# Mirrored row sums, x reversed through DRAM, and a third PSUM bank for the MLP

## The chip, the core and the metric

The kernel runs on one core of one Trainium2 chip. The metric is the device time of one execution in microseconds (us), start to end, as the median of several runs. Profiles are of one execution; their times count from the start of its span. PE is TensorE (matmuls), DVE is VectorE, ACT is ScalarE, POOL is GpSimd, SP is SyncE; the last three also issue DMAs, each from its own queue, in order.

## The reference

A chunked attention is followed by a Fourier mix and an MLP. Batch B = 4, 8 heads, sequence S = 768, head size 64, so 512 columns (DM) per row.

```
for each chunk of 32 rows:                 # keys: 8 memory keys + rows -16..+8 around it
    a = softmax(q_c @ k_full.T / 8);  out[chunk] = a @ v_full
x = out with the heads side by side        # [4, 768, 512]
mixed = real(fft(fft(x, axis=1), axis=2))
u  = x + mixed
un = (u - mean(u)) / sqrt(var(u) + 1e-6)   # over the 512 columns
result = u + relu(un @ w_ch1) @ w_ch2      # w_ch1 [512, 2048], w_ch2 [2048, 512]
```

For a real x, the value of `mixed` at row s and column d equals that at row (768 - s) mod 768 and column (512 - d) mod 512.

## The kernel before

**Tiles.** A batch's x is one SBUF tile `xsb` of 128 partitions x 6 row tiles (st or kt, 0 to 5) x 512 columns, float32. Attention runs in 16 steps, four to a batch, each for two heads: PE turns q and k (`trq`, `trk`, line 313), computes scores in two halves (`sc`, 351), ACT takes the exponential (359), PE the values (`xa`, 372), and DVE divides and writes into `xsb` (`e_norm`, 382 and 383).

**Fourier mix of a batch.** DVE folds x by its symmetries (`e_zy`, `e_pq`, `e_ff`), ACT and DVE split the result into two float16 parts (`e_hi`, `e_lo`), and PE transforms along the sequence into 193 of the frequencies for four parts (`ps`, lines 440 and 534). `e_up` (ACT) and `e_rest` (DVE) copy each part out of PSUM as `up`, in two float16 halves. `e_dn` (DVE, 461) makes a reversed copy `dn` of each part for the row tiles 3 to 5. PE then transforms along the columns, one row tile at a time (`e_columns`, 545): 8 matmuls of 256 columns into one PSUM bank `pm`, from `up` for kt 0 to 2 and from `dn` for kt 3 to 5. `e_sum` (DVE, 551) adds `pm` to x in place, `e_stats` (557, 558) takes mean and variance, `e_un` (ACT, 563) subtracts the mean into a float16 tile, which is transposed into `unT`: by PE in batch 0, by a DMA on SP's queue (`e_flip`, 575) in batches 1 to 3.

**MLP of a batch.** In two halves (sh) of three row tiles: 16 tiles of hidden units `ph` (four matmuls of 384 columns each, 596) go through relu on ACT (`hT`, 603); then for each of the three row tiles 16 matmuls of 512 columns (`pc`, 610, in four parts). `e_osb` (DVE, 616) scales by the row's 1/sigma and adds u, and `e_out` (ACT's queue, 620) stores the 256 KB tile. `e_rstd` (584, 585) computes 1/sigma on POOL.

**PSUM.** Eight banks: one `tr`, two `sc`, one `xa`, two of tag `acc` and two of tag `mlp`. `acc` holds `ps` and `pm`. The MLP's `ph` and `pc` take `mlp` banks in turn; only in the last batch every third of them takes an `acc` bank (`mtag`, 588).

**Order.** All work is handed to a planner (`Plan`, 37) as tasks with an engine, an expected cost, dependences, and the buffers that they take and give back. `order` plays these costs through once, while the program is built, and emits the instructions; on the chip each engine runs its list in that order, with semaphores between engines. MLP matmuls are marked as filler: PE takes them when nothing else is ready. So the Fourier mix and the attention of one batch run between the MLP matmuls of the batch before, and the MLP of batches 2 and 3 is left over at the end. Early on, PE runs `idle` matmuls (654) as a filler.

**Loads.** q and k come on POOL's queue (286) into three buffers each, v on SP's queue (295 to 304) into four, the MLP weights on POOL's queue (786, 790).

Of the kernel before, what the change touches and what calls it, by code (L numbers as in the profile page):

```python
# [10 lines left out]
FP32 = mybir.dt.float32  # L11
# [20 lines left out]
def strided(src, off, dims):  # L32
    return bass.AP(tensor=src.tensor, offset=src.offset + off,
                   ap=[list(src.ap[0])] + [list(d) for d in dims])
# [105 lines left out]
def kernel(  # L140
# [11 lines left out]
    nc = tc.nc  # L152
# [39 lines left out]
    plan = Plan(dict(qs=NS, ks=NS, va=NV, kTb=NKT, qT=2, tr=1, sc=1, xa=1, e1=3,  # L192
                     xsb=3, fold=2, hl=1, up=4, dn=4, acc=2, mlp=2, un=6, unT=2, hT=1, osb=3))
    add = plan.add
# [193 lines left out]

    zy_of, pq_of, ff_of, hl_of, ps_of, up_of, pm_of, un_of, tp_of = ({} for _ in range(9))
    mu_of, unT_of, rstd_of, g_of = {}, {}, {}, {}  # L390
    mid = cpool.tile([P, 2, NST, 1], FP16)
    mid32 = cpool.tile([P, NST, 1], FP32)
    warm = cpool.tile([P, 1], FP32)
    gate = cpool.tile([P, 1], FP32)

# [63 lines left out]
    def e_dn(b, par, ab):  # L459
        dn = fpool.tile([P, 2, HS], FP16, tag="dn", bufs=4, name="dn")  # L460
        nc.vector.tensor_copy(dn, rev_ap(up_of[b, par, ab][2], HS, HS, [[2 * NK, 2]]))
        up_of[b, par, ab][1] = dn

    def g_zy(par, g):
# [84 lines left out]
    def e_sum(b, kt):  # L549
        uv = xs[b][:, kt, :].rearrange("p (j c) -> p c j", c=2)  # L550
        nc.vector.tensor_tensor(uv, pm_of.pop((b, kt)), uv, ALU.add)  # L551

# [19 lines left out]
    def e_flip(b, kt):  # L572
        if kt == 0:
            unT_of[b] = fpool.tile([P, NDT, S], FP16, tag="unT", bufs=2, name="unT")
        nc.sync.dma_start_transpose(unT_of[b][:, :, ts(kt, P)], un_of.pop((b, kt)))

# [9 lines left out]


    def mtag(b, i):
        return "acc" if b == B - 1 and i % 3 == 2 else "mlp"

# [22 lines left out]
    def e_osb(b, sh, stl):  # L613
        st = sh * 3 + stl
        osb_of[b, st] = osb = fpool.tile([P, DM], FP32, tag="osb", bufs=3, name="osb")
        nc.vector.scalar_tensor_tensor(osb, pc_of.pop((b, sh, stl)), rstd_of[b][:, st:st + 1],  # L616
                                       xs[b][:, st, :], ALU.mult, ALU.add)

    def e_out(b, st):
        nc.scalar.dma_start(out[b, ts(st, P), :], osb_of.pop((b, st)))  # L620


    t_zero = add("DVE", 0.2, e_zero, rank=-21)
# [170 lines left out]
    def first_fourier():  # L794
# [38 lines left out]
        return columns_of(0, t_rest)  # L833

    def fourier(b):
        nrm = [[t_norm[b * HP + i, g] for i in ii for g in range(2)] for ii in ((0, 1), (2, 3))]
        t_rest = {}
# [27 lines left out]
    def columns_of(b, t_rest):  # L865
        t_dn = {}
        for par in range(2):
            for ab in range(2):
                t_dn[par, ab] = add("DVE", 0.36, lambda par=par, ab=ab: e_dn(b, par, ab),
                                    [t_rest[par, ab]], take=("dn",))  # L870
        t_un = {}
        allr = list(t_rest.values())
        cols = {}

        def columns(kt):
            cols[kt] = add("PE", 0.9, lambda: e_columns(b, kt),
                           allr + [t_rows] + (list(t_dn.values()) if kt > 2 else []),
                           take=("acc",), rank=len(plan.tasks) + (15 if kt == 3 else 0),
                           give=("up",) * 4 if kt == 2 else ("dn",) * 4 if kt == 5 else ())

        sa = None
        columns(0)
        for kt in range(NST):
            if kt + 1 < NST:
                columns(kt + 1)
            su = add("DVE", 0.7, lambda kt=kt: e_sum(b, kt), [cols[kt]], give=("acc",))
            sa = add("DVE", 0.9, lambda kt=kt: e_stats(b, kt), [su, sa])
            un = add("ACT", 0.72, lambda kt=kt: e_un(b, kt), [sa], take=("un",))
            if b > 0:
                t_un[kt] = add("SP", 0.1, lambda kt=kt: e_flip(b, kt), [un, t_un.get(kt - 1)],  # L890
                               take=("unT",) if kt == 0 else (), give=("un",), moved=0.8,
                               loose=True)
                continue
# [9 lines left out]
    def mlp(b, t_un, rs):  # L903
        for sh in range(2):
            relu = []
            c2 = None
            for ht in range(NHT):
                ph = add("PE", 0.65, lambda sh=sh, ht=ht: e_ch1(b, sh, ht),
                         mlp_prev + [t_un[3 * sh + i] for i in range(3)] + t_w1,
                         take=(mtag(b, ht),), give=("unT",) if sh == 1 and ht == NHT - 1 else (),  # L910
# [5 lines left out]
            for stl in range(3):  # L916
                st = 3 * sh + stl
                for part in range(4):
# [6 lines left out]
                          take=("osb",),   # L925
                          give=(mtag(b, stl), "xsb") if st == NST - 1 else (mtag(b, stl),),
                          rank=RELU(len(plan.tasks)))
                mlp_prev[0] = c2
                add("ACT", 0.1, lambda st=st: e_out(b, st), [os_], give=("osb",), moved=0.9,
                    rank=RELU(len(plan.tasks)))  # L930

    def RELU(i):
        return i - MLPS
# [44 lines left out]
```

## Time and profile before

| | |
|---|---|
| median of 3 runs | 309.21 us (308.92 to 309.44) |
| the profiled execution | 308.85 us, span 307.1 us, granted PE clock 0.999 |
| PE busy | 289.5 us, 3148 matmuls |
| DVE, ACT, POOL busy | 171.2, 161.5, 40.8 us |
| MLP matmuls, ph and pc | 91.6 and 86.9 us of busy PE |
| column matmuls pm | 4 x 9.2 us of busy PE (four groups of 48, 273 ns each) |

The busy time of a matmul runs from its start to its modelled end and overlaps the next one, so the distance from start to start is shorter than the mean duration. A wait is put down to the instruction whose semaphore came last. The time of the profiled execution is its span and what lies around it.

### The profile page before, as it was taken

The page shows a single profiled execution, that of the slowest core. Times are in us where ns is not written, and L with a number is a line of the kernel's source. Part 1 is how long each engine was busy: PE and PEld are TensorE (multiplying, and loading weights), DVE is VectorE, ACT ScalarE, POOL GpSimd, SP SyncE. Part 2 cuts the span into 40 slices and gives each one's busy share as a digit, 9 for nine tenths or more (in the row PEclk, how much of TensorE's full clock was granted, in tenths as well). Part 3 has the DMA queues.
Part 4 walks back from the last instruction along what each step waited for, and adds up shares of the span by engine and source line. Part 5 has one row for each costly group of instructions (what it writes and reads, how often), then busy time and mean ns, then how long its engine had stood idle before and what let it go on. Part 6 is the DMA issues. An engine that isn't in the chain of part 4 may idle for free.

```text
span 307.1 us, 7496 instructions
## 1 busy us (share of the span) xinstructions
PE 289.5 (94%) x3148; PEld 181.5 (59%) x3148; DVE 171.2 (56%) x371; ACT 161.5 (53%) x291; POOL 40.8 (13%) x78
## 2 busy tenths in 40 slices
PE   1399999999999999999989999999999999999994
PEld 1267678866666676666756646675554554554541
DVE  7877895975397887797764399476101001001001
ACT  6656373689884666885257423743360450531710
POOL 8806421132201102000020000000200000000000
PEclk9999999999999999999999999999999999999999
DMA  6989999999944925821361011004201101001011
GB/s 114 197 171 167 204 205 196 198 204 178 193 72 91 203 45 111 136 47 40 89 137 36 2 46 59 0 19 102 86 2 40 64 2 68 34 2 71 31 36 68
DMA packets 60289, 28.93 MB, mean 94 GB/s; under 512 B 48480, under 2 KB 56672, under 8 KB 60256
## 3 DMA queue, kind: packets, MB, share of 16 engines
q1 hardware_dynamic: 47168, 11.61, 21.0%
q0 software_dynamic: 9344, 10.49, 20.8%
q10 hardware_dynamic: 3744, 6.36, 5.7%
q8 instruction: 25, 0.41, 0.5%
q14 instruction: 8, 0.07, 0.1%
HBM read 30.28 MB, written 6.29 MB: 119 GB/s over the span
## 4 chain that ended last, share of the span: by engine, by line
PE 91%; DMA 2%; POOL 2%; DVE 1%; ACT 1%; issue 1%; POOLq 0%; ACTq 0%
PE ph L596 28%; PE pc L610 27%; PE xa L372 9%; PE pm L545 7%; PE ps L440 5%; PE idle L654 5%; PE ps L534 4%; PE sc L351 3%; DMA qs<-in_q_dram 2%; PE trk L313 2%; PE trq L313 2%; DVE osb L616 1%; POOL qs L286 0%; ACT hT L603 0%; PE tp L570 0%
## 5 line engine op out<-in xcount | busy, mean ns | idle before, releaser
L603 ACT ACTIVATE hT<-ph 128x384 f16<-128x384 f32 x128 | 60.9, 492 | 63.0 <-PE ph L596 51.5
L596 PE MATMUL ph<-unT,w_sb 128*128 128x384 f16 x512 | 91.6, 326 | 2.2 <-ACT hT L603 1.1
L610 PE MATMUL pc<-w_sb,hT 128*128 128x512 f16 x384 | 86.9, 379 | 0.0
L596 PEld LDWEIGHTS <-w_sb 128*128 128x128 f16 x512 | 47.8, 97 | 36.8 <-issue 5.7
L616 DVE SCALAR_TENSOR_TENSOR osb<-pc,rstd,xsb 128x512 f32<-128x512 f32 x24 | 18.0, 749 | 82.5 <-PE pc L610 82.4
L610 PEld LDWEIGHTS <-hT 128*128 128x128 f16 x384 | 36.8, 98 | 41.2 <-issue 0.2
L359 ACT ACTIVATE e<-sc,mbias 128x384 f32<-128x384 f32 x64 | 33.8, 583 | 13.8 <-PE sc L351 11.3
L372 PEld LDWEIGHTS xa<-va,e 128*64 128x64 f32 x768 | 25.0, 137 | 7.8 <-issue 7.0
L372 PE MATMUL xa<-va,e 128*64 128x65 f32 x768 | 29.3, 226 | 0.0
L563 ACT ACTIVATE un<-xsb,mu_s 128x512 f16<-128x512 f32 x24 | 17.2, 720 | 14.9 <-DVE mu_s L558 14.8
L382 DVE RECIPROCAL zs<-xa 128x6 f32<-128x6 f32 x32 | 6.1, 191 | 25.6 <-PE xa L372 25.5
L452 ACT CAST up<-ps 128x386 f16<-128x386 f32 x16 | 9.7, 603 | 19.1 <-PE ps L440 13.5
L551 DVE TENSOR_TENSOR xsb<-pm,xsb 128x512 f32<-128x512 f32 x24 | 16.0, 675 | 4.4 <-PE pm L545 4.2
L383 DVE TENSOR_TENSOR xsb<-xa,zs 128x384 f32<-128x384 f32 x32 | 17.8, 557 | 1.1
L557 DVE BATCH_NORM_STATS2 st<-xsb 128x6 f32<-128x512 f32 x24 | 16.4, 684 | 0.5
L654 PE MATMUL idle<-dz 128*128 128x384 bf16 x71 | 15.3, 350 | 1.0 <-DVE zero L230 1.0
L322 ACT COPY qT<-trq 128x768 bf16<-128x768 bf16 x16 | 12.8, 798 | 5.6 <-PE trq L313 5.5
L286 POOL DMA_DIRECT2D ks<-in_k_dram x16 | 10.2, 635 | 35.0 <-PE trk L313 31.4
L584 POOL TENSOR_SCALAR rstd<-mu_s 128x6 f32<-128x6 f32 x4 | 1.0, 245 | 102.0 <-DVE osb L616 57.7
L313 PE MATMUL trq<-ident_b,qs 96*64 96x96 bf16 x256 | 9.4, 221 | 5.1 <-DMA qs<-in_q_dram 5.1
L286 POOL DMA_DIRECT2D qs<-in_q_dram x16 | 10.5, 659 | 25.2 <-PE trq L313 21.5
L456 DVE TENSOR_TENSOR up<-ps,up 128x386 f16<-128x386 f32 x16 | 9.6, 598 | 7.5 <-ACT up L452 7.5
(126 smaller groups left out, 343.5 us busy)
## 6 DMA issues: line engine op xcount, KB each, us to landing
va<-in_v_dram SPq DMA_DIRECT2D x32, 220.0 KB
out_dram<-osb ACTq DMA_DIRECT2D x24, 256.0 KB
w_sb<-in_moe_w_ch_dram POOLq DMA_DIRECT2D x8, 512.0 KB, 16.9
qs<-in_q_dram POOLq DMA_DIRECT2D x16, 192.0 KB, 5.7
ks<-in_k_dram POOLq DMA_DIRECT2D x16, 192.0 KB, 6.1
va<-in_mem_v_dram SPq DMA_DIRECT2D x32, 24.0 KB
va<-in_v_dram SPq DMA_DIRECT2D x32, 22.0 KB
va<-in_v_dram SPq DMA_DIRECT2D x16, 32.0 KB
```

Source lines behind the costliest of these rows:

```text
L286: nc.gpsimd.dma_start(dst[n % NS][0:QP], src[b, 2 * pr:2 * pr + 2].rearrange("h (p j) d -> p h (j d)", j=RB))
L313: nc.tensor.transpose(out_[64 * hh:64 * hh + 64, j * w:(j + 1) * w], src[:, hh, j * D:(j + 1) * D], eye)
L359: nc.scalar.activation(e1[:, :, :, ts(half, 32)], sc[:, :, 0:6, ts(half, 32)], AFT.Exp, bias=mbias[:, half:half + 1], scale=1.0 / math.sqr ...
L372: nc.tensor.matmul(xa[64 * half:64 * half + 64, st, hh, 0:65], e1[:, hh, t6, :], v1[:, hh, 6 * g + t6, 0:65], start=True, stop=True)
L383: nc.vector.tensor_tensor(xs[b][:, 3 * g:3 * g + 3, 2 * pr * D:(2 * pr + 2) * D] .rearrange("p s (h d) -> p s h d", h=2), xa[:, :, :, 0:D] ...
L545: nc.tensor.matmul(pm[:, par, :], lhs, rhs[:, par, :], start=(im == 0), stop=(im == 3))
L563: nc.scalar.activation(un, xs[b][:, kt, :], AFT.Identity, bias=mu_of[b][:, kt, 0:1], scale=-1.0)
L596: nc.tensor.matmul(ph[:, 0:384], w1_sb[:, dt, ts(ht, P)], unT_of[b][:, dt, sh * 384:(sh + 1) * 384], start=(dt == 0), stop=(dt == NDT - 1))
L603: nc.scalar.activation(hT_of[b, sh][:, ht, :], ph_of.pop((b, sh, ht))[:, 0:384], AFT.Relu, bias=0.0, scale=-1.0)
L610: nc.tensor.matmul(pc_of[b, sh, stl], hT_of[b, sh][:, ht, ts(stl, P)], w2_sb[:, ht, :], start=(ht == 0), stop=(ht == NHT - 1))
L616: nc.vector.scalar_tensor_tensor(osb, pc_of.pop((b, sh, stl)), rstd_of[b][:, st:st + 1], xs[b][:, st, :], ALU.mult, ALU.add)
L654: nc.tensor.matmul(fill_of[0][:, 0:384], dz, strided(dz, 0, [[0, 3], [1, P]]), start=True, stop=True)
```

## The change

**Mirrored row sums (batches 1 to 3).** The column transform is done for kt 0 to 2 only, and `e_dn` is gone for these batches. A row tile of the upper half is summed from the `pm` of its mirror, kt - 3, read backwards, and from x, which has been brought into mirrored row order: `e_sum_back` (DVE), a long instruction of 2 x 255 columns and one of two columns. So `xsb` holds the rows 3 to 5 in mirrored order from there on. `e_sum` no longer gives its `acc` bank back; `e_sum_back` of kt + 3 does. The bank's first row is overwritten for row 384, which has no mirror among the first 384, by six matmuls (`e_last_row`) between the sum and the `e_sum_back` of kt 0. The sums run in the order 0, 1, 3, 4, 2, 5.

**x reversed by way of DRAM.** `e_back` writes rows 3 to 5 of `xsb` (786 KB) to a DRAM tensor in reversed partition order, once the batch's last norm is done; `e_mirror` reads it back with four DMAs, shifted by one, into `xr`, which takes the place of `dn`. All five are on POOL's queue.

**Outputs.** The MLP takes the row tiles in the order 0, 3, 4, 5, 1, 2. Tiles 3 to 5 are stored by ACT's queue into a DRAM tensor (`e_out_rows`), and copied from there to their place in mirrored row order by SP's queue (`e_out_back`), with one more DMA for row 384.

**Third bank.** `mtag` gives every third ph or pc tile an `acc` bank in all four batches.

```diff
@@ -190,7 +190,7 @@
     seq = [(b, pr) for b in range(B) for pr in (0, 2, 1, 3)]
 
     plan = Plan(dict(qs=NS, ks=NS, va=NV, kTb=NKT, qT=2, tr=1, sc=1, xa=1, e1=3,
-                     xsb=3, fold=2, hl=1, up=4, dn=4, acc=2, mlp=2, un=6, unT=2, hT=1, osb=3))
+                     xsb=3, fold=2, hl=1, up=4, dn=1, acc=2, mlp=2, un=6, unT=2, hT=1, osb=3))
     add = plan.add
     MLPS = 1000000
 
@@ -386,11 +386,13 @@
             xa[:, :, :, 0:D], zs.unsqueeze(3).to_broadcast([P, 3, 2, D]), ALU.mult)
 
 
-    zy_of, pq_of, ff_of, hl_of, ps_of, up_of, pm_of, un_of, tp_of = ({} for _ in range(9))
+    zy_of, pq_of, ff_of, hl_of, ps_of, up_of, pm_of, un_of, tp_of, dn_of, xr_of = ({} for _ in range(11))
...
+    xd = nc.dram_tensor("x_rows", [2, P, 3, DM], FP32).ap()
+    od = nc.dram_tensor("out_rows", [2, 3, P, DM], FP32).ap()
     gate = cpool.tile([P, 1], FP32)
 
     def e_zy(b, par, c):
@@ -457,9 +459,43 @@
                                 up[:, 0].rearrange("p k s -> p s k"), ALU.subtract)
 
     def e_dn(b, par, ab):
-        dn = fpool.tile([P, 2, HS], FP16, tag="dn", bufs=4, name="dn")
+        if b not in dn_of:
+            dn_of[b] = fpool.tile([P, 4, 2, HS], FP16, tag="dn", bufs=1, name="dn")
+        dn = dn_of[b][:, 2 * par + ab]
         nc.vector.tensor_copy(dn, rev_ap(up_of[b, par, ab][2], HS, HS, [[2 * NK, 2]]))
         up_of[b, par, ab][1] = dn
+
+    def e_back(b):
+        r0 = xd[b % 2, 63:64]
+        nc.gpsimd.dma_start(bass.AP(tensor=r0.tensor, offset=r0.offset,
+                                    ap=[[64 * 3 * DM, 2], [-3 * DM, 64], [1, 3 * DM]]),
+                            xs[b][:, 3:6, :].rearrange("p t d -> p (t d)"))
+
+    def e_mirror(b):
+        xr_of[b] = xr = fpool.tile([P, 3, DM], FP32, tag="dn", bufs=1, name="xr")
+        xb = xd[b % 2]
+        nc.gpsimd.dma_start(xr[1:65], xb[64:128])
+        nc.gpsimd.dma_start(xr[65:128], xb[0:63])
+        nc.gpsimd.dma_start(xr[0:1, 0:2], xb[63:64, 1:3])
+        nc.gpsimd.dma_start(xr[0:1, 2:3], xb[63:64, 0:1])
+
+    def e_last_row(b):
+        pm = pm_of[b, 0]
+        for par in range(2):
+            todo = [(up_of[b, par, ab][0][:, part, HS:HS + 1], (cosD, nsinD)[ab])
+                    for ab in range(2 - par) for part in range(2)]
+            for i, (lhs, rhs) in enumerate(todo):
+                nc.tensor.matmul(pm[0:1, par, :], lhs, rhs[:, par, :], start=(i == 0),
+                                 stop=(i == len(todo) - 1))
+
+    def e_sum_back(b, kt):
+        pm, xr = pm_of.pop((b, kt)), xr_of[b]
+        y = xs[b][:, 3 + kt, :].rearrange("p (j c) -> p c j", c=2)
+        r = xr[:, 2 - kt, :].rearrange("p (j c) -> p c j", c=2)
+        nc.vector.tensor_tensor(y[:, :, 1:HD], strided(pm, HD - 1, [[HD - 1, 2], [-1, HD - 1]]),
+                                r[:, :, 1:HD], ALU.add)
+        nc.vector.tensor_tensor(y[:, :, 0], strided(pm, 0, [[2 * HD - 1, 2]]), r[:, :, 0],
+                                ALU.add)
 
     def g_zy(par, g):
         if g == 0:
@@ -548,7 +584,7 @@
 
     def e_sum(b, kt):
         uv = xs[b][:, kt, :].rearrange("p (j c) -> p c j", c=2)
-        nc.vector.tensor_tensor(uv, pm_of.pop((b, kt)), uv, ALU.add)
+        nc.vector.tensor_tensor(uv, pm_of[b, kt], uv, ALU.add)
 
     def e_stats(b, kt):
         if kt == 0:
@@ -572,7 +608,7 @@
     def e_flip(b, kt):
         if kt == 0:
             unT_of[b] = fpool.tile([P, NDT, S], FP16, tag="unT", bufs=2, name="unT")
-        nc.sync.dma_start_transpose(unT_of[b][:, :, ts(kt, P)], un_of.pop((b, kt)))
+        nc.sync.dma_start_transpose(unT_of[b][:, :, ts(SLOT.index(kt), P)], un_of.pop((b, kt)))
 
     def e_unT(b, kt):
         if kt == 0:
@@ -585,8 +621,13 @@
         nc.gpsimd.tensor_tensor(rstd, rstd, mhalf, ALU.pow)
 
 
+    SLOT = (0, 3, 4, 5, 1, 2)
+
+    def slot(b, i):
+        return SLOT[i] if b else i
+
     def mtag(b, i):
-        return "acc" if b == B - 1 and i % 3 == 2 else "mlp"
+        return "acc" if i % 3 == 2 else "mlp"
 
     ph_of, pc_of, hT_of, osb_of = ({} for _ in range(4))
 
@@ -611,7 +652,7 @@
                              start=(ht == 0), stop=(ht == NHT - 1))
 
     def e_osb(b, sh, stl):
-        st = sh * 3 + stl
+        st = slot(b, sh * 3 + stl)
         osb_of[b, st] = osb = fpool.tile([P, DM], FP32, tag="osb", bufs=3, name="osb")
         nc.vector.scalar_tensor_tensor(osb, pc_of.pop((b, sh, stl)), rstd_of[b][:, st:st + 1],
                                        xs[b][:, st, :], ALU.mult, ALU.add)
@@ -619,6 +660,21 @@
     def e_out(b, st):
         nc.scalar.dma_start(out[b, ts(st, P), :], osb_of.pop((b, st)))
 
+    def e_out_rows(b, st):
+        nc.scalar.dma_start(od[b % 2, st - 3], osb_of.pop((b, st)))
+
+    def e_out_back(b, st):
+        t = st - 3
+        p0 = 1 if t == 0 else 0
+        src, r0 = od[b % 2, t, p0:P, :], S - P * t - p0
+        top = out[b, r0:r0 + 1, :] if r0 < S else out[b, 0:1, :]
+        half = [[1, HD]]
+        nc.sync.dma_start(bass.AP(tensor=top.tensor, offset=top.offset,
+                                  ap=[[HD, 2], [-DM, P - p0]] + half),
+                          bass.AP(tensor=src.tensor, offset=src.offset,
+                                  ap=[[HD, 2], [DM, P - p0]] + half))
+        if p0:
+            nc.sync.dma_start(out[b, HS:HS + 1, :], od[b % 2, 0, 0:1, :])
 
     t_zero = add("DVE", 0.2, e_zero, rank=-21)
     t_table = add("ACT", 1.4, lambda: nc.scalar.activation(warm, zero, AFT.Sin), [t_zero], rank=-3)
@@ -832,7 +888,12 @@
                                               give=(tag,))
         return columns_of(0, t_rest)
 
+    t_xr = {}
+
     def fourier(b):
+        t_x1 = add("POOL", 1.3, lambda: e_back(b), [t_norm[b * HP + i, 1] for i in range(HP)],
+                   moved=2.0)
+        t_xr[b] = add("POOL", 2.4, lambda: e_mirror(b), [t_x1], take=("dn",), moved=2.0)
         nrm = [[t_norm[b * HP + i, g] for i in ii for g in range(2)] for ii in ((0, 1), (2, 3))]
         t_rest = {}
         zy = {}
@@ -863,32 +924,50 @@
         return columns_of(b, t_rest)
 
     def columns_of(b, t_rest):
-        t_dn = {}
-        for par in range(2):
-            for ab in range(2):
-                t_dn[par, ab] = add("DVE", 0.36, lambda par=par, ab=ab: e_dn(b, par, ab),
-                                    [t_rest[par, ab]], take=("dn",))
-        t_un = {}
+        t_dn, t_un, cols = {}, {}, {}
         allr = list(t_rest.values())
-        cols = {}
+        kts, sa = (0, 1, 2, 3, 4, 5), None
+        if b == 0:
+            for par in range(2):
+                for ab in range(2):
+                    t_dn[par, ab] = add("DVE", 0.36, lambda par=par, ab=ab: e_dn(b, par, ab),
+                                        [t_rest[par, ab]],
+                                        take=("dn",) if (par, ab) == (0, 0) else ())
+        else:
+            kts = (0, 1, 3, 4, 2, 5)
 
         def columns(kt):
+            if b > 0 and kt > 2:
+                if kt == 3:
+                    cols[kt] = add("PE", 0.7, lambda: e_last_row(b), [t_sum[0]])
+                return
+            give = (("up",) * 4 if kt == 2 else ("dn",) if kt == 5 else ())
             cols[kt] = add("PE", 0.9, lambda: e_columns(b, kt),
                            allr + [t_rows] + (list(t_dn.values()) if kt > 2 else []),
                            take=("acc",), rank=len(plan.tasks) + (15 if kt == 3 else 0),
-                           give=("up",) * 4 if kt == 2 else ("dn",) * 4 if kt == 5 else ())
-
-        sa = None
-        columns(0)
-        for kt in range(NST):
-            if kt + 1 < NST:
-                columns(kt + 1)
-            su = add("DVE", 0.7, lambda kt=kt: e_sum(b, kt), [cols[kt]], give=("acc",))
+                           give=give)
+
+        t_sum = {}
+        columns(kts[0])
+        for i, kt in enumerate(kts):
+            if i + 1 < NST and not (b > 0 and kts[i + 1] == 3):
+                columns(kts[i + 1])
+            if b == 0 or kt < 3:
+                su = add("DVE", 0.7, lambda kt=kt: e_sum(b, kt), [cols[kt]],
+                         give=("acc",) if b == 0 else ())
+                t_sum[kt] = su
+                if b > 0 and kt == 0:
+                    columns(3)
+            else:
+                su = add("DVE", 0.8, lambda kt=kt: e_sum_back(b, kt - 3),
+                         [cols.get(kt), t_sum[kt - 3], t_xr[b]],
+                         give=("acc", "dn") if kt == 5 else ("acc",))
             sa = add("DVE", 0.9, lambda kt=kt: e_stats(b, kt), [su, sa])
             un = add("ACT", 0.72, lambda kt=kt: e_un(b, kt), [sa], take=("un",))
             if b > 0:
-                t_un[kt] = add("SP", 0.1, lambda kt=kt: e_flip(b, kt), [un, t_un.get(kt - 1)],
-                               take=("unT",) if kt == 0 else (), give=("un",), moved=0.8,
+                t_un[kt] = add("SP", 0.1, lambda kt=kt: e_flip(b, kt),
+                               [un, t_un.get(kts[i - 1]) if i else None],
+                               take=("unT",) if i == 0 else (), give=("un",), moved=0.8,
                                loose=True)
                 continue
             tp = add("PE", 0.26, lambda kt=kt: e_turn_u(b, kt), [un, t_idh], take=("mlp",),
@@ -906,7 +985,7 @@
             c2 = None
             for ht in range(NHT):
                 ph = add("PE", 0.65, lambda sh=sh, ht=ht: e_ch1(b, sh, ht),
-                         mlp_prev + [t_un[3 * sh + i] for i in range(3)] + t_w1,
+                         mlp_prev + [t_un[slot(b, 3 * sh + i)] for i in range(3)] + t_w1,
                          take=(mtag(b, ht),), give=("unT",) if sh == 1 and ht == NHT - 1 else (),
                          rank=MLPS + len(plan.tasks), filler=True)
                 relu.append(add("ACT", 0.5, lambda sh=sh, ht=ht: e_relu(b, sh, ht),
@@ -914,7 +993,7 @@
                                 take=("hT",) if ht == 0 else (), give=(mtag(b, ht),),
                                 rank=RELU(len(plan.tasks))))
             for stl in range(3):
-                st = 3 * sh + stl
+                st, end_b = slot(b, 3 * sh + stl), 3 * sh + stl == NST - 1
                 for part in range(4):
                     end = part == 3
                     c2 = add("PE", 0.88, lambda sh=sh, stl=stl, part=part: e_ch2(b, sh, stl, part),
@@ -923,9 +1002,14 @@
                              rank=MLPS + len(plan.tasks), filler=True)
                 os_ = add("DVE", 0.76, lambda sh=sh, stl=stl: e_osb(b, sh, stl), [c2, rs],
                           take=("osb",), 
-                          give=(mtag(b, stl), "xsb") if st == NST - 1 else (mtag(b, stl),),
+                          give=(mtag(b, stl), "xsb") if end_b else (mtag(b, stl),),
                           rank=RELU(len(plan.tasks)))
                 mlp_prev[0] = c2
+                if b and st > 2:
+                    o1 = add("ACT", 0.1, lambda st=st: e_out_rows(b, st), [os_], give=("osb",),
+                             moved=0.9, late=1.5, rank=RELU(len(plan.tasks)))
+                    add("SP", 0.1, lambda st=st: e_out_back(b, st), [o1], moved=0.9, loose=True)
+                    continue
                 add("ACT", 0.1, lambda st=st: e_out(b, st), [os_], give=("osb",), moved=0.9,
                     rank=RELU(len(plan.tasks)))
 
```

## The prediction

> **What bounds the kernel now.** I read the page first: busy shares, slices, and the chain that ended last.
>
> ```profile
> PE 289.5 (94%) x3148; PEld 181.5 (59%) x3148; DVE 171.2 (56%) x371; ACT 161.5 (53%) x291; POOL 40.8 (13%) x78
> ...
> PE   1399999999999999999989999999999999999994
> ...
> DVE  7877895975397887797764399476101001001001
> ...
> PE 91%; DMA 2%; POOL 2%; DVE 1%; ACT 1%; issue 1%; POOLq 0%; ACTq 0%
> ```
>
> PE is full from the second slice to the last, and the chain runs through PE for 91% of the span. DVE is busy until about 215 us and then nearly idle: from there on only the MLP is left. What counts is therefore PE's own work and PE's waits. The waits of PE, asked for 60 to 262 us only:
>
> ```profile
> PE ph L596 <- ACT hT L603: 1.1, 3, 0.6
> PE ph L596 <- DVE unT L580: 0.7, 1, 0.7
> PE ph L596 <- DVE osb L616: 0.4, 2, 0.2
> ```
>
> All are waits of the MLP's first matmul for a PSUM bank. Matmuls overlap, so what a wait costs is read from start to start (PE's timeline):
>
> ```profile
> 205.69 0.38 PE L545 MATMUL pm<-cosD,dn 128*128 128x256 f16 x2
> ...
> 207.43 1.03 PE L610 MATMUL pc<-w_sb,hT 128*128 128x512 f16 x4
> ...
> 209.17 8.80 PE L610 MATMUL pc<-w_sb,hT 128*128 128x512 f16 x40
> 217.80 0.81 PE L596 MATMUL ph<-unT,w_sb 128*128 128x384 f16 x4
> 218.81 0.97 PE L596 MATMUL ph<-unT,w_sb 128*128 128x384 f16 x5 [0.19 <-DVE osb L616]
> ```
>
> 16 pm matmuls take 207.43 - 205.69 = 1.74 us, 0.109 each; 40 pc 8.63, 0.216 each; a ph takes 0.162 in an undisturbed run. The four ph at 217.80 need 0.65, but the next one starts 1.01 later.
>
> **PE work.** For batches 1 to 3 the columns of row tiles 3, 4 and 5 go: 3 x 3 x 8 = 72 matmuls x 0.109 = 7.85 us. Added are 3 x 6 matmuls of e_last_row. They have one output row, but the same 256 moving columns; the rows with one output (ps<-cosS 128*1, mean 245 ns) last as long as those with 128 (245 ns), so 18 x 0.109 = 1.96. Net **-5.9**. All of it is on the path, since PE has something queued behind every one. Fewer changes between kinds of matmul (about six, 0.05 to 0.10 each by the starts): **-0.4**.
>
> **The third bank.** The MLP now takes an acc bank for every third tile in all batches, not in the last alone. What the two-bank rotation costs, start to start against full rate: before 70.91, behind the copy of unT, 0.84; the 20 ph from 156.15, 4.58 for 3.25, 1.32; the 36 ph from 188.89, 6.65 for 5.85, 0.80; the 64 from 217.80, 0.98, and from 239.54, 1.05. Batch 3, which has the third bank already, loses 0.09 and nothing at the same places (261.34, 282.19). In the changed order I followed each new ph to the relu or sum that frees its bank, and found none of the five waits again: **-4.9**. Sure of it are only the two in the pure MLP stage (2.0), which is the other bound.
>
> **A new wait on the columns.** This is the price. Before, e_sum released the acc bank; now, for batches 1 to 3, kt 0 and 1 keep both acc banks until e_sum_back has read them a second time. Columns of kt 2 wait for the first such release. Who else needs acc: every third MLP tile. DVE's pace is in its timeline:
>
> ```profile
> 202.63 0.69 DVE L551 TENSOR_TENSOR xsb<-pm,xsb 128x512 f32<-128x512 f32 x1 [1.94 <-PE pm L545]
> 203.35 0.69 DVE L557 BATCH_NORM_STATS2 st<-xsb 128x6 f32<-128x512 f32 x1
> 204.08 0.18 DVE L558 BATCH_NORM_AGGREGATE mu_s<-st 128x2 f32<-128x6 f32 x1
> 204.18 0.66 DVE L551 TENSOR_TENSOR xsb<-pm,xsb 128x512 f32<-128x512 f32 x1
> ```
>
> A sum with its statistics takes 1.55, and the first sum starts 1.08 after the first pm (201.55). e_sum_back is not in this trace: its long half has 510 elements from PSUM and a float32 tile, so I take L551's 0.69; its two-element half by the 128x6 copy (L416, 166 ns); together 0.86, bounds 0.7 and 1.1. In batch 3 the changed PE order has kt 0, kt 1, the last row and kt 2 back to back, then the last pc tile, which itself takes acc; no later MLP tile may pass it. From kt 0's start: PE ends kt 1 at 1.74 and the last row at 2.48 (it waits for the first sum until 1.8). DVE: sums at 1.08 and 2.63, sum_back of kt 3 at 4.18 to 5.0. kt 2 starts at 5.05: 2.6 idle. It ends at 5.92; sum_back of kt 4 runs from 5.85 to 6.7, so pc starts 0.75 late. With the 0.1 ahead of the last row **+3.4** (2.8 to 4.2). In batch 1 two attention steps, three ph and a norm on DVE lie between; kt 2 meets a free bank, and ph tile 11 waits for sum_back of kt 5: **+0.5** (0 to 1.5). In batch 2 the filler is longer, and only a late relu shows: **+0.2** (0 to 1). The clock stays: PE is granted full speed until 306.60, 3.4 us after its last matmul, and this gap is shorter.
>
> **DVE, ACT and the queues.** Twelve dn copies go (12 x 0.359 = 4.3), nine small sums come (1.5); DVE has idle time, so nothing beyond the window above. ACT issues 24 output DMAs as before, with no wait on a DMA that is still running.
>
> The mirror runs on POOL: e_back writes 786 KB to DRAM, waits for the batch's last norm; then four DMAs wait for its landing. Behind them on POOL stand k of tile 13, q and k of 14 and 15 (batch 1), and for batches 2 and 3 only rstd. Between the last xa of the batch and its first columns the changed PE order holds 25.8, 25.2 and 23.2 us of matmuls (rates above; an xa group 0.80, a score group 0.23, a transpose group 0.43), and the first sum_back comes 4 to 5 us later: 31, 31 and 27 us of cover. The k of tile 13 is needed 47 us of PE work after e_back. What do the hops cost? Nearest rows:
>
> ```profile
> w_sb<-in_moe_w_ch_dram POOLq DMA_DIRECT2D x8, 512.0 KB, 16.9
> ```
>
> ```profile
> q10 hardware_dynamic: 3744, 6.36, 5.7%
> ```
>
> Low end: q10, the output stores, moves 6.36 MB in 5.7% of 16 engines x 307.1 us, 22.7 KB per us and engine; over 16 engines 786 KB take 2.2, and a q load of 192 KB lands 5.7 after its issue on POOL's queue (page, median), so about 7 a hop. High end: w_sb, eight queued behind each other, 512 KB in 16.9, so 786 KB in 26. Two hops: 14 to 52. I take the low end, as these DMAs stand alone on the queue like a q load: covered, **0**. Uncovered it costs a microsecond of PE for each of delay, in each batch.
>
> [...]
>
> SP gets twelve row copies; those of batch 1 stand ahead of batch 3's flips, which are needed 40 us later. At the end, the two-hop tile is the third from last: its osb ends 6.2 us ahead of the last osb's start (two pc tiles of 3.46, less 0.75). A store lands 1.7 after its issue (303.94 to 305.6), so the copy is issued about 4.4 ahead of the last osb, while the last direct store lands 2.5 behind it: 6.9 of cover for one 256 KB copy. At 16 engines it takes 1.7, hidden; bounds 1.7 and 8.5 (half of w_sb), 0 to 1.6, I take **+0.2**.
>
> **Sum.** The profiled execution took 308.85 (span 307.1 and 1.75 around it); the median of three, 309.21, is 0.36 above. 308.85 - 5.9 - 0.4 - 4.9 + 3.4 + 0.5 + 0.2 + 0.2 = 301.95; in terms of the median **302.3**.
>
> **Rivals.**
> *The mirror is late* (slower). Place: the first e_sum_back, where DVE stands and with it kt 2 and all of PE. It decides when the two hops exceed about 32 us: 1 + 1 + 5 then eat the 6.9. At 34 us: 3 + 3 + 7 = 13 more, 315. For it: two hops through DRAM, w_sb's 16.9. Against: those loads came eight in a row beside full queues, while the DMA engines are busy for 0.38 of the time at 140 to 160 us and 0.12 at 160 to 200 (table by windows). 11%.
> *The shared acc banks give the gain back.* Only the pure MLP's 2.0 is won, and row sums and columns of batches 1 and 2 wait at the upper bounds (1.5 and 1): 302.3 + 2.9 + 1.8 = 307. For it: DVE is 80% busy there. Against: the order puts two to four fillers between. 15%.
> *The last copy ends last.* 2 to 4 us of tail, 304 to 306. 8%.
> *No column wait*, if the pool finds a bank: 298.9. Against: two acc buffers, both held. 4%.
>
> **How the numbers follow.** My forecast has 62%; its own range is 300.8 to 304.5. Taking in most of the second and third rival gives 300.6 to 308. A measurement here can tell about 0.2%, 0.6 us. Faster: the forecast, the second to fourth rival less a margin for steps that I overlooked, 0.86; same 0.03; slower 0.11.
>
> **What would show it.** Right: pm x72 plus 18 one-row pm at PE; between the pm of kt 1 and kt 2 of batch 3 an idle PE of 2.6 us released by DVE's sum_back, and 0.75 ahead of the next pc; ph 0 and 1 of batch 2 without the 0.36 us between them (218.81 less 217.80 and 0.65); no PE or DVE wait put down to a DMA on xr. Wrong: DVE waiting on xr, or the last thing to end being the SP copy; PE idle at ph for acc banks in batch 0 or 1.

## The result, and the profile after

| kernel | median us | runs | ratio to the kernel before | span of the profiled execution |
|---|---|---|---|---|
| before | 309.06 | 4 | 1 | 307.1 |
| after | 336.37 | 4 | 1.0894 (1.0857 to 1.0932) | 334.4 |

The change makes the kernel 27 us slower; the forecast was 302.3 us. In this table and below, an execution that lies over 1.5% above the fastest of the same kernel is left out of median and ratio (four of ten of e4_bank, one of four of e7_after_pool).

The page of the changed kernel, the lines that answer to those shown of before, and the granted clock in 40 slices of 8.36 us:

```profile
PE 286.4 (86%) x3094; PEld 178.0 (53%) x3094; DVE 168.8 (50%) x368; ACT 163.1 (49%) x291; POOL 49.7 (15%) x93
...
PE   1499999999999999900599999996999999999940
...
DVE  8859877952986773840054967957401001020010
...
PEclk9999999999999999955599999998999999999995
...
PE 69%; DMA 12%; DVE 7%; issue 4%; SPq 3%; POOL 1%; ACT 0%; POOLq 0%; DVEq 0%; ACTq 0%
```

PE has two holes that it did not have: slices 18 to 20 (142 to 167 us), with the clock at half, and the last slice. A weaker spot is slice 28, with the clock at 0.8. The three are treated in turn.

**The hole in the middle.** PE's waits, 55 to 335 us:

```profile
PE ph L637 <- DMA unT<-un: 20.9, 1, 20.9
PE pm L581 <- DVE xsb L497: 2.9, 1, 2.9
```

One wait of 20.9 us, of the MLP of batch 1, for its flips (`unT<-un`, the DMAs that transpose `un`). Their instructions are on SP's queue. SP's waits in 120 to 160 us, then the pieces of the chain of waits that lead to the first ph (start, length, what), then the flips in SP's timeline:

```profile
SPq L611 <- DMA out_dram<-osb: 11.0, 1, 11.0
SPq L304 <- DMA out_dram<-osb: 8.0, 1, 8.0
```

```profile
136.90 8.08 DMA out_dram<-osb
...
145.04 1.46 SPq L611
...
148.09 2.61 SPq L295
...
154.33 1.22 SPq L611
...
155.65 6.56 DMA unT<-un
...
162.34 2.72 PE ph L637 x8
```

```profile
132.70 13.80 SPq L611 DMA_TRANSPOSE unT<-un  x2
...
154.33 3.87 SPq L611 DMA_TRANSPOSE unT<-un  x3
```

A flip reads `un` and writes `unT`. It has no business with an output store, and yet SP stands for 11.0 us before the second flip until a store of batch 0, which ACT issued at 136.90, has landed. The link is the completion semaphore. In the trace the DMAs of SP and ACT share eight semaphores (those of POOL have eight others), and each of them goes only after the last step of the one before it on the same semaphore: the store's came at 144.98, and the second flip goes at 145.04. In the changed program the second flip takes the semaphore of that store, and a value load (L304) that of the store before it, which ACT issued at 129.04. ACT can issue a store only when PE has come to that part of batch 0's MLP. So the flips, the first of whose `un` was begun at 113.89, went at 132.70, 145.04, 154.33 and 155.65, with the loads of one value tile (146.6 to 154.2) between the second and third.

In the kernel before, SP had such waits as well, and longer ones. Its row for 110 to 160 us:

```profile
SPq L295 <- DMA out_dram<-osb: 31.0, 3, 13.2
```

They cost nothing there: the three flips that the first half of the MLP needs had gone at 122.14, 123.55 and 129.03, just ahead of the 13.2. The third had landed at 131.70, and PE came to the first ph of batch 1 only at 156.15, 24 us later (the flips, then PE):

```profile
122.14 2.60 SPq L575 DMA_TRANSPOSE unT<-un  x2
...
129.03 1.23 SPq L575 DMA_TRANSPOSE unT<-un  x1
```

```profile
156.15 0.81 PE L596 MATMUL ph<-unT,w_sb 128*128 128x384 f16 x4
```

So both sides have moved: in the changed kernel PE is through with all that stands ahead of that ph at 141.47, 15 us earlier, and the last flip that it needs lands at 162.21, 30 us later.

**The spot at 230 us** is the columns of batch 3. PE's timeline, and the clock by windows (the window, then busy times, and PEclk as the third number from the end):

```profile
228.70 0.38 PE L488 MATMUL pm<-cosD,up 128*1 128x256 f16 x2
231.96 0.39 PE L581 MATMUL pm<-cosD,up 128*128 128x256 f16 x2 [2.88 <-DVE xsb L497]
...
232.53 0.63 PE L581 MATMUL pm<-cosD,up 128*128 128x256 f16 x2
...
233.54 1.01 PE L651 MATMUL pc<-w_sb,hT 128*128 128x512 f16 x2
```

```profile
231.00:232.00 1.00, 0.04 (x1) 0.04 (x2) 0.82 (x3) 0.41 (x1) 0.00 (x0) 1.00 0.00 0
...
233.00:234.00 1.00, 1.00 (x5) 0.43 (x4) 0.97 (x3) 0.60 (x1) 0.00 (x0) 0.50 0.00 0
...
236.00:237.00 1.00, 1.00 (x7) 0.43 (x5) 0.96 (x3) 0.71 (x1) 0.00 (x0) 1.00 0.00 0
```

PE idles 2.88 us for `e_sum_back`, as forecast, and then works at half clock from 232.3 to 235.7, which loses 1.7 us more.

**The tail.** The last matmul ends 13.1 us before the span does; before it was 4.0. SP's waits from 300 us on, and its timeline from 318 us on:

```profile
SPq L672 <- DMA out_rows<-osb: 10.5, 2, 9.4
SPq L672 <- DMA out_dram<-osb: 7.1, 1, 7.1
...
SPq L1057 <- DMA out_dram<-out_rows: 5.7, 1, 5.7
```

```profile
324.97 0.59 SPq L672 DMA_DIRECT2D out_dram<-out_rows  x1
```

The copy of row tile 4 could go after its own first hop (issued at 301.40). It goes at 317.27, because its semaphore was last used by the first hop of tile 5, issued at 315.25. Tile 5's copy has the semaphore of the direct store issued at 318.70, and goes at 324.97. The trace has 16 steps of the semaphore for this store, each with its time: 14 came by 320.69, the last two at 324.58 and 324.95, beside tile 4's copy (317.27 to 327.08). So both copies stand behind each other at the very end.

**Transfers.** In the list of DMA issues (the last number is the median of issue to landing):

```profile
x_rows<-xsb POOLq DMA_DIRECT2D x3, 768.0 KB, 19.9
...
xr<-x_rows POOLq DMA_DIRECT2D x3, 384.0 KB, 5.8
```

Of the 16 steps of the write in batch 2, 14 came by 137.23 and the last two at 153.51 and 153.57. Its 128 packets of 6144 B run from 135.17 to 153.23, two at a time for 15.0 us of it and one for 2.8. Of the store issued at 136.90, 14 came by 139.87 and the last two at 144.43 and 144.98.

### The profile page after: what moved, and what is told of

Read it like the earlier page. It is cut to its first block, busy times and chain, and to the rows that moved or that the text cites. A ratio compares the mean times of both kernels' runs of the same rounds, so it can differ in the third digit from the quotient of the medians.

```text
span 334.4 us, 7427 instructions
## 1 busy us (share of the span) xinstructions
PE 286.4 (86%) x3094; PEld 178.0 (53%) x3094; DVE 168.8 (50%) x368; ACT 163.1 (49%) x291; POOL 49.7 (15%) x93
## 4 chain that ended last, share of the span: by engine, by line
PE 69%; DMA 12%; DVE 7%; issue 4%; SPq 3%; POOL 1%; ACT 0%; POOLq 0%; DVEq 0%; ACTq 0%
PE ph L637 22%; PE pc L651 19%; PE xa L372 7%; DMA x_rows<-xsb 6%; PE idle L710 4%; PE ps L442 3%; PE ps L570 3%; PE pm L581 3%; PE sc L351 2%; DMA out_dram<-osb 2%; PE trk L313 2%; DMA unT<-un 2%; PE trq L313 2%; SPq L295 2%; DMA xr<-x_rows 2%
## 5 line engine op out<-in xcount | busy, mean ns | idle before, releaser
L637 PE MATMUL ph<-unT,w_sb 128*128 128x384 f16 x512 | 90.2, 329 | 20.9 <-DMA unT<-un 20.9
L651 PE MATMUL pc<-w_sb,hT 128*128 128x512 f16 x384 | 87.8, 383 | 0.0
L637 PEld LDWEIGHTS <-w_sb 128*128 128x128 f16 x512 | 48.5, 98 | 54.1 <-DMA unT<-un 21.3
L351 PE MATMUL sc<-qT,kTb 64*128 64x64 bf16 x384 | 11.3, 193 | 2.2 <-DVE kTb L340 2.2
L340 ACT COPY kTb<-trk 128x1056 bf16<-128x1056 bf16 x12 | 12.5, 1040 | 1.0 <-PE trk L313 0.9
## 6 DMA issues: line engine op xcount, KB each, us to landing
x_rows<-xsb POOLq DMA_DIRECT2D x3, 768.0 KB, 19.9
```

The lines of the kernel that those rows point to most:

```text
L351: nc.tensor.matmul(sc[:, hh, t6, :], kT[r0:r0 + 64, t, :], qT[r0:r0 + 64, ts(t, 64)], start=True, stop=True, tile_position=(r0, 0))
L637: nc.tensor.matmul(ph[:, 0:384], w1_sb[:, dt, ts(ht, P)], unT_of[b][:, dt, sh * 384:(sh + 1) * 384], start=(dt == 0), stop=(dt == NDT - 1))
L651: nc.tensor.matmul(pc_of[b, sh, stl], hT_of[b, sh][:, ht, ts(stl, P)], w2_sb[:, ht, :], start=(ht == 0), stop=(ht == NHT - 1))
```

## The experiments

Two things in the profile could have made the flips late: the queue (SP waits on semaphores that ACT's stores hold) and the traffic (batch 2's `e_back` runs from 133.65 to 153.57, with an outermost size of 2 in its pattern; in this time stores, flips and value loads land late). I began with the traffic as the theory ("A") and the queue as the rival ("B").

### e1_back8: the write to x_rows in eight blocks

```
-  ap=[[64 * 3 * DM, 2], [-3 * DM, 64], [1, 3 * DM]]        # from row 63
+  ap=[[16 * 3 * DM, 8], [-3 * DM, 16], [1, 3 * DM]]        # from row 15
   # e_mirror: eight loads of 16 rows instead of two of 64 and 63
```

> The changed kernel, but x is written back to DRAM in eight blocks of 16 rows instead of two of 64, so that the pattern's outermost size is 8; eight loads of 16 rows then fetch it. Theory A (the write itself is the trouble: with an outermost size of 2 it occupies two DMA engines for 19.9 us, and every store, flip and value load that is spread over the engines has a share on those two): the write lands 6 us after its issue or sooner (16 packets x 0.235 = 3.8 us per engine, and about 2 to start and end), the store issued at 136.9 lands after some 2 us instead of 8.1, flip 1 of batch 1 goes before 140, and TensorE's wait of 20.9 us for the flips falls to 0 to 8 us; with the 2.3 us of half clock behind it the time is 313 to 322. Theory B (the order of SyncE's queue is the trouble: flips stand behind value loads and behind semaphores that ScalarE's late stores hold): the wait stays above 15 us and the time above 329. The tail stays as it is under both.

329.92 us, 1.0656 (1.0615 to 1.0698). The wait for the flips fell from 20.9 to 15.2 us only. Wait and time are what theory B asks for (above 15, above 329), though by little; 5.7 us of the wait went with the two-block pattern:

```profile
PE ph L638 <- DMA unT<-un: 15.2, 1, 15.2
```

### e2_out16: the last copy in 16 pieces

```
-  ap=[[HD, 2], [-DM, P - p0], [1, HD]]      # both sides alike
+  ap=[[32, 16], [-DM, P - p0], [1, 32]]
```

> The changed kernel, but the outputs' last copy moves rows in 16 pieces of 32 numbers instead of 2 of 256, so that the outermost size is 16. Theory A: each copy takes 2 to 3 us instead of the 7.7 between the last two on the queue (317.27 and 324.97), the last direct store is no longer slowed, and the tail behind the last matmul falls from 13.1 us towards the 3.9 of the kernel before: 327 (326 to 329); the wait for batch 1's flips stays at 21 us. Theory B (a copy within DRAM that waits for a store within DRAM is slow in itself, latency twice): the tail falls by less than 4 us, 332 or more.

327.98 us, 1.0586 (1.0541 to 1.0631). The tail is 3.8 us (4.0 in the kernel before), and the wait for the flips stays (21.0). But in this build tile 4's copy also has another semaphore and goes at 306.13; pattern and semaphore are told apart in e11 and e12.

### e3_both

Both edits.

> Both edits together. If the two-engine patterns are the whole miss, everything else goes as forecast and the time is 302 to 305. If they are most of it, and the flips of batch 1 still stand 3 to 8 us too late in SyncE's queue, 306 to 313. If the order of the queue is the trouble (theory B), above 320.

321.27 us, 1.0374 (1.0310 to 1.0437), with a wait of 15.3 us for the flips. The write takes 8.7 us instead of 19.9:

```profile
x_rows<-xsb POOLq DMA_DIRECT2D x3, 768.0 KB, 8.7
```

With that, "the two-engine patterns are the whole miss" is ruled out.

### e4_bank: the kernel before with the third bank alone

```
   def mtag(b, i):
-      return "acc" if b == B - 1 and i % 3 == 2 else "mlp"
+      return "acc" if i % 3 == 2 else "mlp"
```

> The kernel before, but every third tile of the MLP takes an acc bank in all batches; nothing else is changed. By the prediction's second step this alone is worth 4.9 us (304.2), of which 2.0 is sure (307.1). By the rival, row sums and columns of batches 1 and 2 wait for the banks that the MLP now holds and give it back: 308.5 to 311.

310.01 us, 1.0000 (0.9960 to 1.0039): no gain. The reason is neither of the two that were expected. PE's only wait after 55 us, and SP's longest in 100 to 160 us:

```profile
PE ph L596 <- DMA unT<-un: 5.0, 1, 5.0
```

```profile
SPq L295 <- DMA out_dram<-osb: 34.6, 4, 23.6
```

No mirror, no DRAM hop, and still the first flip goes at 138.03, the third lands at 149.47, and the MLP of batch 1, ready at 144.55, waits for it. The new order of the work has moved the flips behind a load that waits for one of batch 0's stores. This is theory B without theory A's cause. One of the ten executions took 306.70 us at a granted clock of 1.0, the others 309.92 or more at 0.994 or less; the trace is of one of those, so what was different in that one is not shown.

### e5_nomirror: e3_both without the mirror's transfers

```
-  (e_back: the write to x_rows;  e_mirror: its ten loads)
+  nc.gpsimd.memset(xr, 0.0)
```

> e3_both without any transfer of the mirrored rows: GpSimd fills xr with zeros instead, so the mirrored sums lack x. What is left of the 15.3 us of waiting for batch 1's flips is then not the work of these transfers. Theory A (the x_rows traffic delays stores, flips and value loads): the wait falls to 3 us or less, 306 to 308. Theory B (SyncE's queue stands behind semaphores that ScalarE's output stores of batch 0 give back only at about 131 and 139 us, as TensorE reaches them; the traffic only adds to it): flip 0 still goes at about 133.5, flip 1 at 140, the fourth at 146 or 147, the wait is 6 to 10 us, 311 to 315.

314.09 us, 1.0151 (1.0094 to 1.0208). The wait is 9.0 us with none of the mirror's traffic (the first line of PE's waits below); the first two flips go at 133.68 and 139.95, the third at 147.54. So the queue alone makes 9.0; the mirror's transfers in eight blocks bring it to 15.3, those in two to 20.9.

```profile
PE ph L630 <- DMA unT<-un: 9.0, 1, 9.0
PE pm L574 <- DVE xsb L490: 2.3, 1, 2.3
```

### e6_pool and e7_after_pool: batch 0's stores on GpSimd

```
   def e_out(b, st):
-      nc.scalar.dma_start(out[b, ts(st, P), :], osb_of.pop((b, st)))
+      (nc.scalar if b else nc.gpsimd).dma_start(out[b, ts(st, P), :], osb_of.pop((b, st)))
   # and the task's engine in the plan: "ACT" if b else "POOL"
```

> e3_both with the six output stores of batch 0 issued by GpSimd instead of ScalarE, so that no DMA of SyncE waits for one of them; the mirror's transfers stay. Theory B: flips 0 to 2 go within a few us of their un (115 to 123), the wait of 15.3 us goes altogether, and with it the half clock: 303 to 306. Theory A: the traffic is the same, flips 2 and 3 stay beside it, the wait is still above 8 us and the time above 313.

> The changed kernel, two-engine patterns and all, with only the six output stores of batch 0 moved to GpSimd. Theory B: the wait of 20.9 us for the flips falls to 5 or less, since the flips are out before batch 2's x is written back at 133.7; what stays is the tail of 13.1 us: 336.4 - 21 - 2.3 = 313 (311 to 317). Theory A: two engines stay taken for 19.9 us, the wait stays above 12 us, 327 or more.

e6_pool (on e3_both): 303.21 us, 0.9799 (0.9766 to 0.9832). e7_after_pool (on the changed kernel): 313.49 us, 1.0132 (1.0076 to 1.0188). In both the wait for the flips is gone. In e7_after_pool the write in two blocks still runs from 134.49 to 153.2, but five of the six flips are out before it begins, the three for the MLP's first half among them (SP's timeline):

```profile
119.22 4.13 SPq L611 DMA_TRANSPOSE unT<-un  x2
...
127.28 3.85 SPq L611 DMA_TRANSPOSE unT<-un  x3
```

Its PE waits show the second, smaller price of the slow write. DVE waits 1.8 us for `xr` in batch 3, and PE's gap there is longer:

```profile
PE pm L581 <- DVE xsb L497: 4.8, 2, 4.2
```

### e8_bank_pool and e10_before_pool

The same edit (batch 0's stores on GpSimd) on e4_bank, and on the kernel before.

> The kernel before with the third bank (e4_bank) and batch 0's output stores on GpSimd. In e4_bank SyncE stood from 113.4 to 137.6 and TensorE waited 5.0 us for the flips. If that wait ate the bank's gain, this kernel shows it: 304 to 306. If the gain was never there (row sums and columns wait for banks), 308.5 to 311 as e4_bank.

> The kernel before with batch 0's output stores on GpSimd and nothing else. SyncE's queue then never waits for them, but in the kernel before TensorE did not wait for a flip. If the gain of e8_bank_pool (304.6) is the bank's, this one is at 309 (308.3 to 309.8). If the move of the stores is itself worth something, 305 to 307.

e8_bank_pool: 304.62 us, 0.9847 (0.9773 to 0.9921), with no wait of PE after 55 us. e10_before_pool: 308.57 us, 0.9989 (0.9973 to 1.0004). Moving the stores is worth next to nothing by itself; with the third bank it lets the bank's gain appear, 4.0 us between these two medians.

### e9_spare: other banks for batch 3's columns

On e6_pool:

```
   def e_columns(b, kt):
+      if b == B - 1 and kt in (1, 2):    # the two banks of sc, free by then
+          if kt == 1:
+              spare_of[0] = aps.tile([P, 2, 8, 64], FP32, tag="sc", bufs=1, name="sp")
+          pm = spare_of[0][:, kt - 1].rearrange("p (a j) d -> p a (j d)", a=2)
   # and in the plan what these tasks take and give back: sc instead of acc
```

> e6_pool, and batch 3's columns of row tiles 1 and 2 go to the two PSUM banks of the attention scores, which are free by then, instead of to acc; so tile 2 need not wait for a sum_back, and the pc tile after it finds an acc bank. If the price of the columns in batch 3 is the bank (2.6 us of idle TensorE in e6_pool) and the half clock that follows it there (3.4 us at 0.5, 1.7 lost), both go: 303.2 - 2.6 - 1.7 = 298.9 (298.3 to 300). If the half clock has another cause, only 2.6 goes: 300.6. If VectorE's sums are the limit themselves and the wait moves to the last row or to pc, 302 to 303.5.

299.34 us, 0.9692 (0.9671 to 0.9712), the fastest of all: e6_pool's 303.21 less 3.9. PE waits for nothing after 55 us, and the clock stays:

```profile
PE   1389999999999999999999999999999999999994
...
PEclk9999999999999999999999999999999999999999
```

### e11_narrow_out and e12_narrow_pool: the tail

e11_narrow_out is e9_spare with e2_out16's edit undone. e12_narrow_pool has, besides, the copies on GpSimd:

```
-  nc.sync.dma_start(bass.AP(tensor=top.tensor, ...    # and the copy of row 384
+  nc.gpsimd.dma_start(bass.AP(tensor=top.tensor, ...
```

> e9_spare with the outputs' last copies in 2 pieces of 256 numbers again, on SyncE as in the changed kernel, where the copy of the last batch's tile 4 waits for the first hop of tile 5, whose semaphore it reuses. The tail of 13.1 us comes back (12.5 in e7_after_pool): 299.3 + 8.5 = 307.8 (306.5 to 309.5). If the tail came from the flips' delay and not from the copies, 299 to 301.

> As e11_narrow_out, but the last copies are on GpSimd's queue, whose DMAs have semaphores of their own; each copy still has two pieces and two engines. Theory C (the narrow copy harms because the shared semaphore holds tile 4's copy back until tile 5's, so that two of 7.7 us each run one after the other at the end): tile 4's copy goes some 12 us earlier, tile 5's alone stays at the end, tail 4 to 6 us, 299.3 to 301.5. Theory D (two taken engines slow the last direct stores in any case): tail above 8 us, 303.5 or more.

e11_narrow_out: 308.76 us, 0.9979 (0.9956 to 1.0002), tail 12.9 us. e12_narrow_pool: 302.81 us, 0.9784 (0.9755 to 0.9814). The time lies between the two theories; the tail of 8.5 us is theory D's (above 8). Tile 4's copy goes at 279.04 instead of 289.44 and has landed before tile 5's goes at 288.84, as theory C has it. But a copy still takes 8.5 us in the median:

```profile
out_dram<-out_rows POOLq DMA_DIRECT2D x6, 256.0 KB, 8.5
```

Tile 5's takes 10.4, to 299.25, and of the last direct store, issued at 293.12, 14 of the 16 steps came by 295.11 and the last two at 299.00 and 299.08, as theory D has it. That keeps the tail 4.3 us longer than e9_spare's, which is 4.2. So of the 8.7 us that e11_narrow_out's tail is longer, about half (12.9 - 8.5) goes with the shared semaphore and half stays with the narrow pattern. The semaphore and the move to another queue are not told apart here.

## Why the prediction was wrong, step by step

The profiled execution of after took 336.13 us, the sum had said 301.95. The difference of 34.2 is in three places: the flips, 20.9 and 2.5 of half clock behind them (162.3 to 166 at 0.50, then 2 us at 0.65); the tail, 13.1 - 4.0 - 0.2 = 8.9; the columns, 2.9 + 1.7 - 3.4 = 1.2. Together 33.5; 0.7 is not assigned.

- **"ACT issues 24 output DMAs as before, with no wait on a DMA that is still running" and "SP gets twelve row copies": the step that failed.** It looked at what the queues get, not at who waits for whom. The flips were not moved in the diff, so the prediction gave them no line at all. In the run the second flip stood 11.0 us behind one of those output DMAs, and PE 20.9 us behind the flips; with batch 0's stores on another queue and nothing else changed, the wait is gone (336.4 to 313.5). That the flips had been early enough, by 24 us, was a property of the old order; the new order changed the semaphore that each one takes, and brought PE to their reader 15 us sooner. No rival held this mechanism: "the mirror is late" had the right side and a DMA as the cause, but put the wait on DVE at `xr`, where it was 1.1 us in all.
- **Third bank, -4.9: right in size, on a condition.** With the flips free it is worth 4.0 us (e8_bank_pool against e10_before_pool; the interval of e8_bank_pool alone is over 4 us wide). Without, it is worth nothing (e4_bank): PE comes to batch 1's first ph at 144.55 instead of 156.15, and the third flip lands at 149.47 instead of 131.70. The prediction followed each ph "to the relu or sum that frees its bank", but not to its second input. Of its 4.9, 0.84 was not the wait for a bank that it was called but one for the copy of `unT`; e8_bank_pool shows no wait of PE after 55 us, so this one went as well. In after, the long run of ph in batch 2 that lost 0.98 before goes in one piece, 10.49 us from start to start, against 64 x 0.162 = 10.37:

```profile
238.04 10.65 PE L637 MATMUL ph<-unT,w_sb 128*128 128x384 f16 x64
248.53 1.67 PE L651 MATMUL pc<-w_sb,hT 128*128 128x512 f16 x7
```

- **PE work, -5.9 and -0.4: right, as far as the runs can tell.** The count is 3148 - 72 + 18 = 3094, and the one-row pm start 0.22 apart by two, like the others (228.48 and 228.70). e9_spare, where none of the new waits is left, lies 5.3 us under e8_bank_pool; 6.3 less the 0.7 set aside for batches 1 and 2 would be 5.6. The interval of e8_bank_pool is as wide as this difference.
- **Wait on the columns, batch 3, +3.4: right in place and nearly in size, wrong in its parts.** The gap came where it was put (2.9 and in e6_pool 2.6, forecast 2.6). The 0.75 ahead of pc did not come (e5_nomirror alone shows 0.5). In its stead the clock went to half, against "the clock stays". DVE's steps fit: L495 and L497 took 0.67 and 0.15, forecast 0.69 and 0.17. e9_spare took the price away, 3.9. For batches 1 and 2 (+0.5, +0.2) no wait of PE shows.
- **The mirror, "covered, 0": nearly right, by luck.** Two hops took 19.9 + 5.8, and the first sum_back of batch 3 came 27.0 after its write was issued, as forecast. "I take the low end" of 14 to 52 was wrong: the two took about 26, which left no margin. What the step lacked was the harm to others: beside it, the store of 136.90 took 8.1 us. The last store of the kernel before took 2.0 (303.94 to 305.96; the prediction had 1.7).
- **Tail, +0.2: mis-sized; it is 9.1 longer.** One copy was thought of, with 6.9 us of cover. There were two in a row, since tile 4's copy waits for the semaphore that tile 5's first hop holds. These two took 9.8 and 8.5 us, at or over the upper end that was given (8.5), not the 1.7 taken. The rival "the last copy ends last" was true, and its 2 to 4 us too little.

With the flips freed and both patterns spread, e6_pool measures 303.21 where the prediction said 302.3. The steps on PE, DVE and PSUM hold together; those on the DMA queues did not.

**The outermost size.** The low end of the forecast spreads the write over 16 engines, 2.2 us; it took 19.9 with an outermost 2 and 8.7 with 8 (e3_both). In the packet records of after a packet of 6144 B takes 0.235 us in the median; 64 of them one after the other would take 15.0 and 16 of them 3.8 (an estimate from that median), which leaves the same 4.9 for the rest. Of the write's 16 semaphore steps two came late with an outermost 2 (by 16 us), and eight with 8 (in e3_both eight by 137.96, eight from 141.21 to 142.74). This program waits before it uses a semaphore again, and the runs show what the waiting can cost: 11.0 us ahead of the second flip in after.

## What to carry to other kernels

A queue that waits is a risk even where it harms nobody: look in the profile for the rows in which a queue waits for a transfer whose data it does not use (31 us here), and ask who stands behind it once the order moves. Before counting the gain of a removed wait, follow the same instruction to its other inputs, since the new order can make one of them late that had 24 us to spare. Give a transfer through DRAM an outermost size that spreads it (the write took 19.9 us with 2 and 8.7 with 8), and put stores whose time depends on the matmuls on a queue that shares no semaphores with loads that must be early (batch 0's stores on GpSimd: 336.4 to 313.5 us).

## What the runs showed of the hardware that I had not expected

- A gap of PE of 2.6 us (e6_pool) or 2.9 us (after) was enough for half clock. In e6_pool the clock fell 2.5 us after the last matmul's end; in after 3.2 (229.1 to 232.3), when PE was already at work again, and in its hole in the middle 2.1 (141.47 to 143.53). The stretch at half clock behind the columns of after lasted 3.41 us (232.27 to 235.68), and others were multiples of that: 6.83 in e2_out16, 10.24 in e5_nomirror, and 23.89 in the middle of after.
- In these runs a DMA landed later beside one with which it shares no data. The same store landed 8.1 us after its issue beside the write in two blocks (after), 5.6 us beside that in eight (e3_both, 137.81 to 143.44), and 2.1 us with no write (e5_nomirror, 137.87 to 139.95), each time read from its issue to the flip that waits for it. In after it was two of its 16 semaphore steps that came late.
- Left open: the MLP's first half in batch 1 now needs the first, third and fourth flip instead of the first three (`SLOT`). No run changed that order alone. In after the third flip landed at 161.56 and the fourth at 162.21, so as the flips went there, the old order would have saved less than a microsecond of the 20.9.
